# A spectral filter before a mixture of experts: another factoring of the 2496-point transform, and the complex filter product moved out of the third stage's matmul

## The chip, the cores and the metric

The kernel runs on one core of a Trainium2 chip. Times are device microseconds of a whole execution; the median of several executions is the figure. A profile is one execution recorded by the hardware; its span goes from the first to the last recorded instruction and is shorter than the device time.

## The reference, cut to what matters

```python
batch, seq, dim = (8, 2496, 256)          # x; filt_r, filt_i are (1249, 256)
X = np.fft.rfft(x, axis=1)
F = (filt_r + 1j * filt_i)[None, :, :]
y = np.fft.irfft(X * F, n=x.shape[1], axis=1).astype(np.float32)

x = y.reshape(8 * 2496, 256)              # 19968 tokens, 8 experts, F = 1024
logits = x @ w_gate
expert_idx = np.argmax(logits, axis=1)
probs = softmax(logits)                   # gate_w = the chosen expert's
out[n] = gate_w[n] * (np.maximum(x[n] @ w1[e], 0) @ w2[e])    # e = expert_idx[n]
```

Everything is float32.

## The kernel before, in words

It has two halves: the transform with the routing (the first 970 us of the profile), and the experts (the rest). The change is in the first half.

The transform of one batch is written as four stages of matrices. With n = 26 q + t, stage A (`stage_a`, L253) takes 96-point transforms over q, for 26 columns t, two columns (512 numbers a row) to a matmul. Its result goes to a DRAM buffer `zd` and comes back with other rows: 104 = 26 t by 4. Stage B (L266) is a 104 by 104 matrix for each of 24 slots p, 256 columns wide, which gives the coefficients X (real and imaginary parts are rows). VectorE then multiplies X by both parts of the filter, `ht`, in one instruction for a pair of slots (L270, 104 rows by 1024 numbers: P = X Fr and Q = X Fi). Stage C (L281, for the first pair L277) is the back transform over 26 points. It takes P and Q as two matmuls that add up in PSUM, so the complex product's additions and sign changes lie in its matrices, and TensorE does twice the work of one product. ScalarE copies the result out (L282), it goes to the DRAM buffer `ud`, and comes back as 96 rows for stage D (L296), a matrix for each of the 26 columns. D's result `yo` goes to DRAM (`yd`, L312), is transposed on TensorE (L302) and multiplied with the gate weights (L310). When a batch has all its gate products, `route` finds expert, gate and row on VectorE with two matmuls between (L346, L347), and GpSimd scatters (token, gate) to a table in DRAM, one indirect DMA per column: 26 per batch (L368).

A column pair's copies out of PSUM go to ScalarE and VectorE in turn (`evac`, L186 and L188).

The stages of three batches run together: in round b stage B and C of batch b, A of batch b+1 and D of batch b-1, a chunk of four columns or four slots of each in turn (`run_all`). `route` of batch b-1 stands at the end of round b. The program's order on each engine is set when it is built, by a scheduler that estimates times; on the chip every engine takes its own list in order. All loads and stores of the transform are issued by SP; a DMA waits, besides its data, for the DMA issued eight before it on that queue. Input tiles (xt, zi, ui) share 7 buffers, output tiles 5, PSUM banks of the matmuls 5.

The first A chunk is loaded ahead of the constants, the other six behind them: tables, filter (`load_filters`, which copies half of `ht` to its other partitions by DMA, L215), and a fill of the table (L241).

The experts take 128 tokens of one expert at a time: gather by GpSimd (L453), transposes, two matmul layers, a scatter of the result (L502). The first load of the table (L445) waits for all scatters of the routing.

Of the kernel before, what the change touches and what calls it, by code (L numbers as in the profile page):

```python
# [10 lines left out]
F32 = mybir.dt.float32  # L11
# [11 lines left out]
E = 8  # L23
F = 1024
# n = N2*q + t, k = f + N1*g
N1 = 96
N2 = 26
G = N2 // 2
NP = N1 // 4
K2 = 4 * N2  # L30
# [4 lines left out]
def dft_tables():  # L35
    """Matrices of the four transform stages; they depend on the shapes alone.

    Slot s = 24*h + p holds the frequency f = s (0 < s < 48) of the length-96 transforms, and slot 0
    the two real ones, f = 0 and f = 48. A slot's 26 coefficients of the whole transform are at
    k = f + 96*g (u = 0) and k = (96 - f) + 96*g (u = 1), g < 13: all have k <= S/2.  # L40
    """
    q = np.arange(N1)
    t = np.arange(N2)
    g = np.arange(G)
    w = 2.0 * np.pi

    ta = np.zeros((N1, 2, 2, NP))
    td = np.zeros((2, 2, NP, N2, N1))
    n = N2 * q[None, :] + t[:, None]
    for s in range(2 * NP):  # L50
        h, p = divmod(s, NP)
        if s == 0:
            ta[:, h, 0, p] = 1.0
            ta[:, h, 1, p] = (-1.0) ** q
            td[h, 0, p] = 1.0
            td[h, 1, p] = (-1.0) ** q[None, :]
        else:
            ang = w * ((q * s) % N1) / N1
            ta[:, h, 0, p] = np.cos(ang)
            ta[:, h, 1, p] = -np.sin(ang)  # L60
            ang = w * ((n * s) % S) / S
            td[h, 0, p] = np.cos(ang)
            td[h, 1, p] = -np.sin(ang)
    td *= 2.0 / S

    # rows (t, h, c), columns (c', h', u, g)
    tb = np.zeros((N2, 2, 2, NP, 2, 2, 2, G))
    for s in range(2 * NP):
        h, p = divmod(s, NP)
        for u in range(2):  # L70
            k = ((N1 - s if s else N1 // 2) if u else s) + N1 * g
            ang = w * ((t[:, None] * k[None, :]) % S) / S
            c, sn = np.cos(ang), np.sin(ang)
            if s == 0:
                tb[:, h, u, p, 0, h, u] = c
                tb[:, h, u, p, 1, h, u] = -sn
            else:
                i = -1.0 if u else 1.0
                tb[:, h, 0, p, 0, h, u] = c
                tb[:, h, 1, p, 0, h, u] = i * sn  # L80
                tb[:, h, 0, p, 1, h, u] = -sn
                tb[:, h, 1, p, 1, h, u] = i * c
    tb[:, 0, :, 0, 1, 0, 0, 0] = 0.0
    tb[:, 0, 0, 0, 1, 0, 0, 0] = (-1.0) ** t

    # rows (c', h', u, g), columns (t, h, c): of Y itself, generic and with slot 0 in h = 0
    y = np.zeros((2, 2, 2, 2, G, N2, 2, 2))
    for z in range(2):
        for h in range(2):
            for u in range(2):  # L90
                if z and h == 0:
                    k = (N1 // 2 if u else 0) + N1 * g
                    ang = w * ((k[:, None] * t[None, :]) % S) / S
                    y[z, 0, h, u, :, :, h, u] = np.cos(ang)
                    y[z, 1, h, u, :, :, h, u] = -np.sin(ang)
                    if u == 0:
                        y[z, 0, h, u, 0, :, h, u] = 0.5
                        y[z, 1, h, u, 0, :, h, u] = 0.5 * (-1.0) ** t
                else:
                    ang = w * (((g[:, None] + u) * t[None, :]) % N2) / N2  # L100
                    i = -1.0 if u else 1.0
                    y[z, 0, h, u, :, :, h, 0] = np.cos(ang)
                    y[z, 1, h, u, :, :, h, 0] = -np.sin(ang)
                    y[z, 0, h, u, :, :, h, 1] = i * np.sin(ang)
                    y[z, 1, h, u, :, :, h, 1] = i * np.cos(ang)
    # of P = X*Fr and Q = X*Fi, with Yr = Pr - Qi and Yi = Pi + Qr
    yq = np.stack([y[:, 1], -y[:, 0]], axis=1)
    yq[1, :, 0, 0, 0] = 0.0
    tc = np.stack([y, yq], axis=1).reshape(4, K2, K2).transpose(1, 0, 2)

    return {
        "ta": ta.reshape(N1, N1),
        "tb": tb.reshape(K2, NP, K2),
        "tc": tc,
        "td": td.reshape(N1, N2, N1),
    }


@with_exitstack
def kernel(  # L120
# [3 lines left out]
    filt_r: bass.AP,  # L124
    filt_i: bass.AP,
# [6 lines left out]
    td: bass.AP,  # L132
    out: bass.AP,
# [3 lines left out]
    B = x.shape[0]  # L137
    N = B * S
# [5 lines left out]
    zd = [dram.tile([N2, 4, NP, D], F32, tag=f"z{b % 2}", name="zd") for b in range(B)]  # L144
    ud = [dram.tile([N2, 4, NP, D], F32, tag=f"u{b % 2}", name="ud") for b in range(B)]
    yd = dram.tile([N + 1, D], F32, tag="yd", name="yd")
    # Expert e's tokens, in any order, from row e*N on: (token, gate); unused rows hold token N.
# [5 lines left out]
    cnt = perm.tile([N1, E], F32, name="cnt")  # L153
    em8 = perm.tile([N1, E], F32, name="em8")
    eoff = perm.tile([N1, E], F32, name="eoff")
# [8 lines left out]
    tas = cst.tile([N1, N1], F32, name="tas")  # L164
    tbs = cst.tile([K2, NP, K2], F32, name="tbs")
    tcs = cst.tile([K2, 4, K2], F32, name="tcs")
    tds = cst.tile([N1, N2, N1], F32, name="tds")
    ht = cst.tile([K2, 2, NP, D], F32, name="ht")
    wg = cst.tile([P, DH, E], F32, name="wg")
    tri = cst.tile([N1, N1], F32, name="tri")  # L170
    ones = cst.tile([N1, N1], F32, name="ones")
    seg = cst.tile([N1, E, N2], F32, name="seg")
    fill = cst.tile([P, 64, 2], I32, name="fill")
    zrow = cst.tile([1, D], F32, name="zrow")
    ids0 = cst.tile([N1, N2], I32, name="ids0")
    e_i = cst.tile([N1, E], I32, name="e_i")
# [13 lines left out]
    xv = x.rearrange("b (q t) d -> b q t d", t=N2)  # L190
    CH = [(t0, min(4, N2 - t0)) for t0 in range(0, N2, 4)]
    PH = [(p0, 4) for p0 in range(0, NP, 4)]

# [1 line left out]
    nc.sync.dma_start(out=tas, in_=ta)  # L195

    def load_filters():
        nc.sync.dma_start(out=tbs, in_=tb)
        for s, f in enumerate((filt_r, filt_i)):
            for h in range(2):  # L200
                r = 26 * h
                nc.sync.dma_start(
                    out=ht[r:r + G, s],
                    in_=bass.AP(f.tensor, f.offset + NP * h * D, [[N1 * D, G], [D, NP], [1, D]]),
                )
                p0 = 1 - h
                nc.sync.dma_start(
                    out=ht[r + G:r + 2 * G, s, p0:],
                    in_=bass.AP(f.tensor, f.offset + (N1 - NP * h - p0) * D, [[N1 * D, G], [-D, NP - p0], [1, D]]),
                )  # L210
            nc.sync.dma_start(
                out=ht[G:2 * G, s, 0:1],
                in_=bass.AP(f.tensor, f.offset + N1 // 2 * D, [[N1 * D, G], [D, 1], [1, D]]),
            )
            nc.sync.dma_start(out=ht[2 * N2:K2, s], in_=ht[0:2 * N2, s])  # L215
            nc.sync.dma_start(out=ht[2 * N2:2 * N2 + 1, s, 0, :], in_=f[S // 2:S // 2 + 1, :])
        nc.sync.dma_start(out=tcs, in_=tcm)
        nc.sync.dma_start(out=tds, in_=td)
        nc.sync.dma_start(out=wg, in_=moe_w_gate.rearrange("(i p) e -> p i e", p=P))

# [3 lines left out]
        out=tri, in_=ones, compare_op=ALU.is_gt, fill=0.0, base=0, pattern=[[1, N1]], channel_multiplier=-1  # L224
# [6 lines left out]
    nc.gpsimd.iota(ids0, pattern=[[1, N2]], base=0, channel_multiplier=N2)  # L231
# [14 lines left out]
    def stage_a(b):  # L246
        for t0, n in CH:
            xt = sb.tile([N1, 4, D], F32, tag="in", name="xt", bufs=7)
            nc.sync.dma_start(out=xt[:, :n], in_=xv[b, :, t0:t0 + n, :])
            zo = sb.tile([N1, 4, D], F32, tag="st", name="zo", bufs=5)  # L250
            for j in range(0, n, 2):
                ps = bank()
                mm(ps[:N1, :], lhsT=tas, rhs=xt[:, j:j + 2, :], start=True, stop=True)  # L253
                evac(zo[:, j:j + 2, :], ps[:N1, :].rearrange("p (t d) -> p t d", t=2))
            nc.sync.dma_start(out=zd[b].rearrange("t a p d -> (a p) t d")[:, t0:t0 + n, :], in_=zo[:, :n])
            yield

    def stage_bc(b):
        for p0, n in PH:
            zi = sb.tile([K2, 4, D], F32, tag="in", name="zi", bufs=7)  # L260
            nc.sync.dma_start(out=zi[:, :n], in_=zd[b].rearrange("t a p d -> (t a) p d")[:, p0:p0 + n, :])
            uo = sb.tile([K2, 4, D], F32, tag="st", name="uo", bufs=5)
            for j in range(0, n, 2):
                ps = bank()
# [246 lines left out]
    with tc.manual_schedule():  # L511
        for i in range(NT + 5):
# [8 lines left out]
            if 5 <= i:  # L521
                result(i - 5)


_INS = ['x', 'filt_r', 'filt_i', 'moe_w_gate', 'moe_w1', 'moe_w2']


# [18 lines left out]
```

## Time and profile before

| | us |
|---|---|
| median of 3 runs | 2474.87 (2455.88 to 2485.93) |
| span of the profiled execution | 2287.2 (no device time of its own is given; the median is 187.7 above it) |
| first matmul of stage B | 94.7 |
| routing matmuls L346 of batches 0 to 7 | 267.1, 373.1, 478.1, 584.6, 689.7, 798.9, 886.8, 916.8 |
| first transpose of the experts | 970.6 |
| TensorE, VectorE, ScalarE, GpSimd busy | 2006.8, 562.6, 417.6, 519.0 |

The rows of the transform that the change touches, from the groups of instructions (mean of one; a matmul of 512 float32 columns is recorded as two instructions):

| line | operation | count | mean ns |
|---|---|---|---|
| L253 | A, 96x512 | 208 | 706 |
| L266 | B, 104x256 | 384 | 473 |
| L270 | product, VectorE, 104x1024 | 96 | 1225 |
| L281 | C, 104x512 | 352 | 778 |
| L282 | copy, ScalarE, 104x512 | 96 | 586 |
| L296 | D, 96x256 | 416 | 385 |
| L302, L310 | transposes; gate products | 416; 832 | 258; 228 |
| L368 | scatter, GpSimd | 208 | 928 |

How to read it: engines are PE (TensorE), DVE (VectorE), ACT (ScalarE), POOL (GpSimd), SP (issues DMAs). In a list in order of time a line has start, length, engine, source line, operation, tile written and tiles read, and in brackets the idle time of that engine just before, with what ended it. In a table of waits a line has who waited for whom, microseconds in total, times, and the longest. PEclk is the clock granted to TensorE, as a share of full speed.

### The profile page before, as it was taken

The page shows a single profiled execution, that of the slowest core. Times are in us where ns is not written, and L with a number is a line of the kernel's source. Part 1 is how long each engine was busy: PE and PEld are TensorE (multiplying, and loading weights), DVE is VectorE, ACT ScalarE, POOL GpSimd, SP SyncE. Part 2 cuts the span into 40 slices and gives each one's busy share as a digit, 9 for nine tenths or more (in the row PEclk, how much of TensorE's full clock was granted, in tenths as well). Part 3 has the DMA queues.
Part 4 walks back from the last instruction along what each step waited for, and adds up shares of the span by engine and source line. Part 5 has one row for each costly group of instructions (what it writes and reads, how often), then busy time and mean ns, then how long its engine had stood idle before and what let it go on. Part 6 is the DMA issues. An engine that isn't in the chain of part 4 may idle for free. (4 is left out here: it accounts for less than half of the span.)

```text
span 2287.2 us, 25424 instructions
## 1 busy us (share of the span) xinstructions
PE 2006.8 (88%) x8246; PEld 1303.9 (57%) x8246; DVE 562.6 (25%) x911; ACT 417.6 (18%) x750; POOL 519.0 (23%) x550
## 2 busy tenths in 40 slices
PE   0468888888888888099999999999999999999998
PEld 0224444444444446066667776667777667777666
DVE  0122323232323233222222222222222222222221
ACT  0112111111211112012222222222222222222221
POOL 0000122130404042622222222222222222222221
PEclk9898779877977788599999999999999999999999
DMA  8875556563837354611111111111111111111110
GB/s 145 231 222 164 135 155 150 144 158 111 185 113 177 112 128 122 154 32 33 34 36 33 32 33 33 34 36 33 32 33 33 33 35 32 33 33 33 35 34 15
DMA packets 127074, 191.90 MB, mean 84 GB/s; under 512 B 41687, under 2 KB 93603, under 8 KB 126596
## 3 DMA queue, kind: packets, MB, share of 16 engines
q1 hardware_dynamic: 104648, 148.28, 25.9%
q0 software_dynamic: 22304, 42.01, 5.8%
q8 instruction: 75, 1.23, 0.2%
q14 instruction: 47, 0.39, 0.1%
HBM read 104.42 MB, written 84.15 MB: 82 GB/s over the span
## 5 line engine op out<-in xcount | busy, mean ns | idle before, releaser
L475 PE MATMUL hps<-w1s,xT 128*128 x1304 | 589.7, 595 | 1.0 <-DMA idt<-table 0.9
L499 PE MATMUL yps<-w2s,hT 128*128 x2608 | 589.6, 379 | 0.3 <-ACT hT L493 0.3
L499 PEld LDWEIGHTS yps<-w2s,hT 128*128 128x128 f32 x2608 | 495.4, 190 | 137.0 <-issue 77.0
L502 POOL DMA_INDIRECT out_dram<-ys,idt x163 | 165.7, 1016 | 933.4 <-ACT ys L501 933.4
L475 PEld LDWEIGHTS hps<-w1s,xT 128*128 128x128 f32 x1304 | 236.1, 191 | 237.2 <-issue 235.9
L368 POOL DMA_INDIRECT table<-pay,row x208 | 193.1, 928 | 766.5 <-DVE row L365 430.4
L281 PE MATMUL bank<-pq,tcs 104*104 104x512 f32 x352 | 226.6, 778 | 84.1 <-DVE pq L270 84.1
L479 DVE TENSOR_SCALAR h<-hps 128x512 f32<-128x512 f32 x163 | 112.8, 692 | 452.6 <-PE hps L475 452.6
L501 ACT ACTIVATE ys<-yps,idt 128x256 f32<-128x256 f32 x163 | 77.4, 475 | 736.3 <-PE yps L499 736.3
L464 DVE COPY xT<-pt 128x256 f32<-128x256 f32 x163 | 69.2, 425 | 505.7 <-PE pt L462 468.0
L270 DVE TENSOR_TENSOR pq<-bank,ht 104x1024 f32<-104x1024 f32 x96 | 117.6, 1225 | 268.6 <-PE bank L266 253.2
L253 PE MATMUL bank<-xt,tas 96*96 96x512 f32 x208 | 119.3, 706 | 65.5 <-DMA xt<-in_x_dram 65.5
L453 POOL DMA_INDIRECT xg<-yd,idt x163 | 158.2, 971 | 60.2 <-issue 53.0
L489 PE MATMUL pt<-ident,h 128*128 128x128 f32 x1304 | 169.2, 273 | 0.1
L281 PEld LDWEIGHTS bank<-pq,tcs 104*104 104x104 f32 x352 | 63.7, 203 | 176.8 <-DVE pq L270 113.5
L481 ACT ACTIVATE h<-hps 128x512 f32<-128x512 f32 x163 | 97.3, 597 | 317.1 <-PE hps L475 317.1
L266 PE MATMUL bank<-zi,tbs 104*104 104x256 f32 x384 | 133.7, 473 | 22.8 <-DMA zi<-zd 22.8
L282 ACT COPY uo<-bank 104x512 f32<-104x512 f32 x96 | 56.3, 586 | 501.5 <-PE bank L281 395.8
L489 PEld LDWEIGHTS pt<-ident,h 128*128 128x128 f32 x1304 | 147.5, 141 | 0.6 <-DVE h L479 0.4
L491 DVE COPY hT<-pt 128x512 f32<-128x512 f32 x163 | 112.8, 692 | 88.1 <-PE pt L489 88.1
L266 PEld LDWEIGHTS bank<-zi,tbs 104*104 104x104 f32 x384 | 78.9, 218 | 77.8 <-issue 60.8
L253 PEld LDWEIGHTS bank<-xt,tas 96*96 96x96 f32 x208 | 40.5, 198 | 136.0 <-issue 66.2
(76 smaller groups left out, 961.2 us busy)
## 6 DMA issues: line engine op xcount, KB each, us to landing
zi<-zd SPq DMA_DIRECT2D x48, 416.0 KB
ud<-uo SPq DMA_DIRECT2D x48, 416.0 KB
xt<-in_x_dram SPq DMA_DIRECT2D x48, 384.0 KB
zd<-zo SPq DMA_DIRECT2D x48, 384.0 KB
ui<-ud SPq DMA_DIRECT2D x48, 384.0 KB
yd<-yo SPq DMA_DIRECT2D x48, 384.0 KB
w1s<-in_moe_w_dram SPq DMA_DIRECT2D x8, 1024.0 KB
w2s<-in_moe_w_dram SPq DMA_DIRECT2D x8, 1024.0 KB
```

What stands on the lines that cost most here:

```text
L253: mm(ps[:N1, :], lhsT=tas, rhs=xt[:, j:j + 2, :], start=True, stop=True)
L266: mm(ps[:K2, i * D:(i + 1) * D], lhsT=tbs[:, p0 + j + i, :], rhs=zi[:, j + i, :], start=True, stop=True)
L270: nc.vector.tensor_mul(pq, z2[:, None].to_broadcast((K2, 2, 2, D)), ht[:, :, p0 + j:p0 + j + 2, :])
L281: mm(ps[:K2, :], lhsT=tcs[:, s, :], rhs=pq[:, s], start=(s == 0), stop=(s == 1))
L368: sc = nc.gpsimd.indirect_dma_start(out=table, out_offset=bass.IndirectOffsetOnAxis(ap=row[:, t:t + 1], axis=0), in_=pay[:, t, :], in_offs ...
L453: nc.gpsimd.indirect_dma_start(out=xg, out_offset=None, in_=yd, in_offset=bass.IndirectOffsetOnAxis(ap=idt[i].bitcast(U32)[:, 0:1], axis=0))
L475: mm(ps, lhsT=xT[:, dh, :], rhs=w1s[:, bass.ds(ev, 1), dh, fh * 512:(fh + 1) * 512], start=(dh == 0), stop=(dh == DH - 1))
L479: nc.vector.tensor_scalar_max(o, ps, 0.0)
L489: nc.tensor.transpose(pt[:, j, :], h[:, (k + j) * P:(k + j + 1) * P], ident)
L491: nc.vector.tensor_copy(hs[i][:, k:k + 4, :], pt)
L499: mm(ps, lhsT=hT[:, ft, :], rhs=w2s[:, bass.ds(ev, 1), ft, :], start=(ft == 0), stop=(ft == FT - 1))
L502: nc.gpsimd.indirect_dma_start(out=out, out_offset=bass.IndirectOffsetOnAxis(ap=idt.pop(i).bitcast(U32)[:, 0:1], axis=0), in_=ys, in_offse ...
```

## The change

2496 is split as 39 times 64 instead of 96 times 26. With n = 64 q + t, stage A is a 39-point transform, and one matrix of 117 rows does three columns t at once (columns start at T0 = 0, 22 and 43; a group has 22, 21 and 21 of them), so a batch has 22 column groups instead of 26 columns, and 11 matmuls. B has 20 slots (frequencies 0 to 19) instead of 24, with 128 rows: 64 t by real and imaginary part. D is a 117 by 117 matrix for each of 22 groups. The table is scattered to in 22 indirect DMAs per batch, of 117 rows (the last of 39).

The filter product is made whole before stage C: VectorE multiplies with the real part (128 rows by 512 numbers), then crosswise with the imaginary part in two instructions of 64 rows each (imaginary half to real half and back; the sign is in the filter table), and GpSimd adds the two. C is then one matmul of 512 columns for a pair of slots.

x and the filter come in a layout made beforehand on the host: x as (8, 128, 22, 256), rows 117 to 127 unused; the filter as one table of (2, 128, 20, 256), which is loaded in four pieces without copies between partitions. Token numbers and a mask for the empty columns are loaded too.

Loads and stores that go by column groups are cut in three (`columns`: 39 rows each), those by slots in two (64 rows each). Per batch SP issues 6 + 18 + 10 + 10 + 18 + 18 = 80 DMAs (x, zd, zi, ud, ui, yd) instead of 40.

```diff
-N1 = 96
-N2 = 26
+N1 = 39
+N2 = 64
+NF = (N1 + 1) // 2
+T0 = (0, 22, 43)
+NB = len(T0)
+NG = 22
+TP = NB * N1
...
+    def columns(ap, i0, n):
+        for j in range(NB):
+            m = min(n, NC[j] - i0)
+            if m > 0:
+                yield slice(j * N1, (j + 1) * N1), m, ap[T0[j] + i0:T0[j] + i0 + m].rearrange("t s d -> s t d")
...
     def stage_a(b):
-            nc.sync.dma_start(out=xt[:, :n], in_=xv[b, :, t0:t0 + n, :])
+            nc.sync.dma_start(out=xt[:, :n], in_=x[b, :, i0:i0 + n, :])
...
-                mm(ps[:N1, :], lhsT=tas, rhs=xt[:, j:j + 2, :], start=True, stop=True)
+                mm(ps[:TP, :], lhsT=tas, rhs=xt[:TP, j:j + 2, :], start=True, stop=True)
...
-            nc.sync.dma_start(out=zd[b].rearrange("t a p d -> (a p) t d")[:, t0:t0 + n, :], in_=zo[:, :n])
+            for r, m, v in columns(zd[b], i0, n):
+                nc.sync.dma_start(out=v, in_=zo[r, :m])
...
     def stage_bc(b):
-            nc.sync.dma_start(out=zi[:, :n], in_=zd[b].rearrange("t a p d -> (t a) p d")[:, p0:p0 + n, :])
+            nc.sync.dma_start(out=zi[:HP, :n], in_=zd[b][:, f0:f0 + n, :])
+            nc.sync.dma_start(out=zi[HP:, z0:n], in_=zd[b][:, NF - 1 + f0 + z0:NF - 1 + f0 + n, :])
...
-                pq = sb.tile([K2, 2, 2, D], F32, tag="pq", name="pq")
-                nc.vector.tensor_mul(
-                    pq, z2[:, None].to_broadcast((K2, 2, 2, D)), ht[:, :, p0 + j:p0 + j + 2, :]
-                )
+                yv = sb.tile([P, 2, D], F32, tag="yv", name="yv")
+                yw = sb.tile([P, 2, D], F32, tag="yw", name="yw")
+                nc.vector.tensor_mul(yv, z2, ht[:, 0, f:f + 2, :])
+                nc.vector.tensor_mul(yw[:HP], z2[HP:], ht[:HP, 1, f:f + 2, :])
+                nc.vector.tensor_mul(yw[HP:], z2[:HP], ht[HP:, 1, f:f + 2, :])
+                ys = sb.tile([P, 2, D], F32, tag="ysum", name="ysum")
+                nc.gpsimd.tensor_tensor(ys, yv, yw, op=ALU.add)
                 ps = bank()
...
-                    for s in range(2):
-                        mm(ps[:K2, :], lhsT=tcs[:, s, :], rhs=pq[:, s], start=(s == 0), stop=(s == 1))
+                    mm(ps, lhsT=tcs[:, 1, :], rhs=ys, start=True, stop=True)
...
-            nc.sync.dma_start(out=ud[b].rearrange("t a p d -> (t a) p d")[:, p0:p0 + n, :], in_=uo[:, :n])
+            nc.sync.dma_start(out=ud[b][:, f0:f0 + n, :], in_=uo[:HP, :n])
+            nc.sync.dma_start(out=ud[b][:, NF - 1 + f0 + z0:NF - 1 + f0 + n, :], in_=uo[HP:, z0:n])
...
     def stage_d(b):
-            nc.sync.dma_start(out=ui[:, :n], in_=ud[b].rearrange("t a p d -> (a p) t d")[:, t0:t0 + n, :])
+            for r, m, v in columns(ud[b], i0, n):
+                nc.sync.dma_start(out=ui[r, :m], in_=v)
...
-                    mm(ps[:N1, i * D:(i + 1) * D], lhsT=tds[:, t0 + j + i, :], rhs=ui[:, j + i, :],
+                    mm(ps[:k, i * D:(i + 1) * D], lhsT=tds[:k, i0 + j + i, :k], rhs=ui[:k, j + i, :],
...
-            nc.sync.dma_start(out=ytok[:, t0:t0 + n, :], in_=yo[:, :n])
+            for r, m, v in columns(ytok, i0, n):
+                nc.sync.dma_start(out=v, in_=yo[r, :m])
...
     def route(b, lgr):
+        nc.vector.tensor_tensor(idx, idx, vld, op=ALU.mult)
...
-        for t in range(N2):
+        for t in range(NG):
+            k = N1 if t == NG - 1 else TP
             sc = nc.gpsimd.indirect_dma_start(
                 out=table,
-                out_offset=bass.IndirectOffsetOnAxis(ap=row[:, t:t + 1], axis=0),
-                in_=pay[:, t, :],
+                out_offset=bass.IndirectOffsetOnAxis(ap=row[:k, t:t + 1], axis=0),
+                in_=pay[:k, t, :],
```

As built, the order on the engines that the prediction speaks of is this. On TensorE a chunk still reads: C of the second pair, two matmuls of A, four of D, transposes and gate products with the next chunk's B between them, C of the first pair, B of the second pair, C of the second pair. On GpSimd the lists of adds and scatters are: 20 adds, 22 scatters, 11 adds, 22 scatters, 10, 22, 9, 22, 10, 22, 10, 22, 10, 22, and the last 22 scatters. Before, GpSimd had scatters alone.

## The prediction

> **What bounds the kernel now.** I read the page's first two parts, then busy time by stretches, then the table of waits, and then the instructions in order of time inside one round of the transform.
>
> ```profile
> span 2287.2 us, 25424 instructions
> ...
> PE 2006.8 (88%) x8246; PEld 1303.9 (57%) x8246; DVE 562.6 (25%) x911; ACT 417.6 (18%) x750; POOL 519.0 (23%) x550
> ...
> PE   0468888888888888099999999999999999999998
> ...
> PEclk9898779877977788599999999999999999999999
> ```
>
> TensorE is the busy engine in both halves. From slice 17 on it runs the experts at 99% and full clock; nothing there is touched. What can move lies in slices 0 to 16, where it is busy 8 tenths and its granted clock lies between 0.7 and 0.9. Columns below: stretch, length, busy time of each engine, granted clock, DMA share, GB/s.
>
> ```profile
> 168.00:267.00 99.00, 82.91 (x334) 46.47 (x334) 28.45 (x39) 18.95 (x33) 0.00 (x0) 0.84 0.51 150
> 268.00:373.00 105.00, 89.10 (x337) 48.17 (x335) 33.37 (x49) 17.23 (x32) 24.10 (x26) 0.79 0.57 147
> ...
> 917.00:970.00 53.00, 1.47 (x4) 0.73 (x4) 9.77 (x24) 0.00 (x0) 33.67 (x37) 0.50 0.69 161
> ```
>
> One round (B and C of one batch, A of the next, D of the one before) is some 105 us: the routing matmuls (L346) start at 267.1, 373.1, 478.1, 584.6, 689.7, 798.9, 886.8 and 916.8, so rounds 2 to 6 take 106.3 each, round 7, without A, 88, round 8, D alone, 30. DMA is half idle; TensorE stands still for 16 us of a round. The waits say for what:
>
> ```profile
> POOL table L368 <- DVE row L365: 430.4, 7, 77.2
> ...
> PE bank L281 <- DVE pq L270: 84.1, 73, 1.4
> ```
>
> So of 96 pairs of slots 73 make TensorE wait for the product. In order of time this is:
>
> ```profile
> 499.21 0.92 POOL L368 DMA_INDIRECT table<-pay,row  x1 [0.30 <-issue]
> ...
> 500.44 0.92 POOL L368 DMA_INDIRECT table<-pay,row  x1 [0.30 <-issue]
> ...
> 515.22 1.91 PE L266 MATMUL bank<-zi,tbs 104*104 104x256 f32 x4
> ...
> 517.17 1.22 DVE L270 TENSOR_TENSOR pq<-bank,ht 104x1024 f32<-104x1024 f32 x1 [6.67 <-PE bank L266]
> ...
> 518.45 3.74 PE L281 MATMUL bank<-pq,tcs 104*104 104x512 f32 x4 [1.32 <-DVE pq L270]
> ...
> 521.98 3.40 PE L253 MATMUL bank<-xt,tas 96*96 96x512 f32 x4
> ...
> 525.22 1.89 PE L296 MATMUL bank<-ui,tds 96*96 96x256 f32 x8
> ...
> 536.55 1.96 PE L281 MATMUL bank<-pq,tcs 104*104 104x512 f32 x4 [1.32 <-DVE pq L270]
> ```
>
> Three things to see. TensorE takes its list in order: behind L266 of a chunk's second pair comes L281 of the same pair with nothing between, so the wait (1.32) is the product (1.22) and a hop. The same work comes in two speeds: L281 3.74 or 1.96, L266 1.91 (1.03 at 527.5), L253 3.40 or 1.88: half and full clock. And a scatter costs GpSimd 1.226 us from start to start (0.92 and 0.30).
>
> **The change, part by part.** I work per round (one batch through each stage), because the rounds repeat, and against the profiled span. The page gives that execution no time but its span, 2287.2; the median run, 2474.87, lies 187.7 above it (the runs 168.7 to 198.7). I carry the 187.7 over unchanged.
>
> **TensorE's work.** A goes from 13 to 11 matmuls of 512 columns (0.94 each), B from 24 to 20 of 256 (0.5), C from 24 to 10 of 512 (0.9), D from 26 to 22 of 256 (0.47), transposes and gate products from 52 to 44 each (0.14 and 0.2). At full clock a round loses 1.9 + 2.0 + 12.6 + 1.9 + 1.1 + 1.6 = 21 us.
>
> **The wait per pair.** The one product of 1.22 becomes three of 512 columns on VectorE and an add on GpSimd, one behind the other. A 512-column VectorE pass from PSUM is 0.69 (L188, L479), and two in a row take 1.50, so three take 2.3. No add on GpSimd is in the trace. Its nearest rows are memsets, 172 ns for 96 elements and 276 for 208: 0.93 ns an element and 83 ns. One stream of 512 elements would be 0.56, three 1.5; I take the two inputs, 1.04. With hops of 0.03 to 0.28 (iota to VectorE, VectorE to scatter) the chain is 3.6 (3.1 to 4.1). The new kernel's list on TensorE has the same shape: the second pair's C stands directly behind its B, so it waits all 3.6; the first pair's has a gate product and its wait in between (1.2), so 2.4.
>
> Only a page prices such an add: the Trainium skill, "GPSIMD Engine Reference", section 3.1, has 4497 ns for 2048 fp32 elements, an estimate of 1.12 for 512, which would add 0.08 a pair, some 6 us in all.
>
> **The scatters in front of the add.** Until now GpSimd had nothing in the transform but scatters, and no one waited for them before the end. Now its list is 20 adds, 22 scatters, 11 adds, 22 scatters, and so on. The scatters of batch b stand before the adds of batch b+2, and TensorE, with C next in its list, stands behind those. From the routing matmul to the row numbers is 5.3 (267.1 to 272.5 without the product that lay between), then 0.28, 22 scatters at 1.226 = 27.0, the add and its hop 1.2: 33.8; TensorE has the routing matmuls and B (3.4) in it. It stands still 30.4 us, in rounds 2 to 7. Queued behind it are A and D of that round; on SP, the stores of their results. Where the first pair's add gets ahead of the scatters, the second is caught: the same.
>
> **One chunk (two pairs, four columns of A and D).** C, A, D in one stretch: 0.9 + 1.88 + 1.89 = 4.7 at full clock, 8.7 at half. Transposes, gate products and the next B: 4.0 (507.8 to 511.7 now), 6.5 at half. Wait 2.4. C and B: 1.9 or 3.7. Wait 3.6. Sum 16.6 at full clock, 24.7 at half. Which clock? In the trace the clock falls after the stretch of transposes and gate products though its gaps are 0.7 at most, holds in round 0 (0.95 from 95 to 160 us) with waits of 1.32 in every 4 to 6 us, and comes back only when a stretch has run dense for some 4 to 6.8 us (530.8 to 535.3; 518.45 to 525.2). Waits of 2.4 and 3.6 around 1.9 of work will drop it in nearly every chunk. I let C, A, D start slow for 5.1 us (then 2.1 more: 7.2) and C and B be slow half the time (2.8): 7.2 + 4.0 + 2.4 + 2.8 + 3.6 = 20.0. Now a chunk takes 17.1.
>
> The rule for this clock speaks against the change as well: the Trainium skill, "TensorE: Matmul & The Clock Gate", section "HAM oscillation — how this bites in real kernels", wants no idle gap over about 3.4 us. The trace is stricter, since it drops the clock with gaps of 0.7; by the page alone only the wait of 3.6 would count, a chunk would be 19.1, and the whole some 32 us less.
>
> **Rounds 2 to 6.** Five chunks 100, less one wait of 2.4, plus 30.4, plus 5.5 for the odd columns and route (10.9 now from the last D to the routing, less a regular 5.4), plus 3.4 for routing and B: 137, against 106.3: +31 each, +155. Round 7, without A on both sides: +35. Round 1, no scatters ahead: 109 against 99.3, +10. Round 0: five chunks of B, wait, C twice and A are 12.9 at full and 18.1 at half clock; with 0.9 and the 9.2 that the loads cost now, 75 to 101 against 73.1; I take 91, +18.
>
> **Ends.** SP waits over 30 us on copies inside the filter load (L215, L216; 120 to 180 GB/s move meanwhile); the new load is 8.4 MB in long rows without such waits, and the rows of 66 to 95 us show 234 to 295 GB/s: the inputs of A come at 35 to 45 instead of 66. Bounds 0 and -32, I take -20. At the end GpSimd issues 44 scatters instead of 52 from 893.4 on, which is what the 53 us of the third stretch are made of: -9 (-6 if a scatter of 117 rows is slower).
>
> **DMA.** SP issues 80 transfers a round instead of 40, of half the size, 0.3 to 0.6 us each; 40 more are 16 us of SP, which is idle most of a round. But each waits for the one issued eight before, and in the list the third load of some ui comes behind stores of the same chunk's zo: D waits 3 to 5 us (at 264.2 a load of zi took 5.0 from issue to use). One such per round is 4 x 7 = +28; bounds 0 and +70. VectorE's two products more per pair (80 x 0.85 = 68 us) cost nothing beside the chain: VectorE is busy 33 of 105; what of them is on the path is in the chain already. Nothing is counted for the padded rows of x (128 rows of 22 columns instead of 2496: +0.3 MB a round, DMA being half idle), the sign change of the filter at the start (behind the load) and one more small product in the routing (0.17 a round).
>
> Sum: 155 + 35 + 10 + 18 - 20 - 9 + 28 = +217. 2474.87 + 217 = 2692, say 2690. All at full clock, no DMA wait, the cheap add: +3; all at half clock, the dear add, all DMA waits: +500.
>
> **Rivals.** (1) TensorE's work is the bound and the waits hide. For it: TensorE is at 85% in a round. Against: its list has nothing to put between B and C. It would give 2475 - 8 x 21 - 29 = 2278. It decides if the waits of a round grow by less than 25 us; I count 5 x 3.6 + 4 x 2.4 + 30 = 58 against 12 now, so they grow by 46. (2) The clock holds: work dense enough at 4.7 us a stretch to get back to full at once: +41, 2516. For it: round 0 holds it today. Against: its waits are 1.32. (3) The clock stays down, and SP's order costs several waits a round: 2840 and up to 2930. For it: the third stretch shows 0.50 when TensorE idles, and C, A, D must be unbroken to win it back; a late ui breaks it.
>
> **How the numbers follow.** My forecast (2570 to 2840) 0.70; rival 2 (2500 to 2570) 0.10; rival 3 (2840 to 2970) 0.13; rival 1 0.07. About 2% is what a measurement of this kernel can tell from no change, 2425 to 2524. Rival 1 complete is faster, 0.03; partly, within 2%, 0.04, and 0.01 of rival 2's lower end. Slower 0.92. For 8 in 10 the range goes half way into rivals 2 and 3 (0.05 each): 2535 to 2880.
>
> **What would show it.** The add's row at 1.0 to 1.1 us; a wait of TensorE for it of 450 us in all (80 times, 2 to 4 each, six of about 30); six groups of GpSimd's 22 scatters, each with TensorE idle beside it; L306 at 80 to 90 matmuls with half the present busy time of C; a clock near 0.7 in slices 2 to 16; first B near 75 us. Wrong if GpSimd's scatters run beside adds, if the long waits are not there, or if the clock in a round is above 0.85.

## The result, and the profile after

| | before | changed |
|---|---|---|
| median, us | 2465.38 (2454.81 to 2485.93, 4 runs) | 2679.77 (2677.44 to 2682.56, 4 runs) |
| ratio | 1 | 1.0861, 95% interval 1.0804 to 1.0918: slower |
| profiled execution | span 2287.2, no time of its own | time 2682.56, span 2680.9 |

Forecast: 2690. The number is right, in part by luck, as the account below shows. The last row does not fit the forecast's frame: the changed kernel's span lies 1.7 us below its time, so nothing like 187.7 us lies around a span, and by the two profiles the kernel lost 394 us, not 214. That had to be settled first (experiment 1).

The page of the changed kernel, its first two parts:

```profile
span 2680.9 us, 25028 instructions
...
PE 1975.8 (74%) x7654; PEld 1307.4 (49%) x7654; DVE 601.0 (22%) x1057; ACT 397.6 (15%) x718; POOL 599.8 (22%) x597
...
PE   2555356454645536365369999999999999999998
...
PEclk6666666665656656566579999999999999999999
```

TensorE went from 8 tenths to 5 in the transform and its clock from 0.7-0.9 to 0.6. It does less work and is hardly less busy. Rounds 2 to 6 of the changed kernel in one stretch (length, busy time of PE, PEld, DVE, ACT, POOL, clock, DMA share, GB/s):

```profile
307.00:1099.00 792.00, 413.52 (x1320) 239.16 (x1320) 185.71 (x341) 78.31 (x142) 171.02 (x160) 0.62 0.40 102
```

and the same rounds in the first profile of before:

```profile
267.00:799.00 532.00, 452.66 (x1691) 248.21 (x1692) 165.16 (x255) 89.59 (x162) 119.86 (x130) 0.79 0.59 145
```

That is 158.5 us a round for 106.4, TensorE busy 82.7 of it for 90.5, where 21 us less was worked out at full clock. What TensorE waits for (who for whom, us in total, times, longest):

```profile
PE bank L306 <- POOL ysum L300: 227.5, 70, 3.7
PE bank L304 <- issue: 90.2, 3, 30.1
...
PE bank L306 <- issue: 51.6, 2, 25.8
PE bank L304 <- POOL ysum L300: 46.3, 5, 30.2
```

All four lines are the wait of C for the sum, 416 us; "issue" stands where the profile names no releaser. The long waits, of 25 us and more, are called holds below. The start of round 2 in order of time, with the end of the row of scatters:

```profile
312.45 0.68 DVE L298 TENSOR_TENSOR yw<-bank,ht 64x512 f32<-64x512 f32 x1
...
337.40 0.98 POOL L410 DMA_INDIRECT table<-pay,row  x1 [0.30 <-issue]
338.69 0.90 POOL L410 DMA_INDIRECT table<-pay,row  x1 [0.30 <-issue]
339.61 1.27 POOL L300 TENSOR_TENSOR ysum<-yv,yw 128x512 f32<-128x512 f32 x1
...
340.93 2.08 PE L304 MATMUL bank<-ysum,tcs 128*128 128x256 f32 x4 [30.24 <-POOL ysum L300]
```

The products are done at 313.1; the add starts at 339.6, behind 22 scatters, and TensorE stands still for 30.24. The groups of GpSimd:

```profile
L300 POOL TENSOR_TENSOR ysum<-yv,yw 128x512 f32<-128x512 f32 x80 | 100.9, 1261 | 845.9 <-DVE yw L298 824.0
...
L410 POOL DMA_INDIRECT table<-pay,row x176 | 173.8, 987 | 176.4 <-DVE row L406 125.2
```

### The profile page after: what moved, and what is told of

It reads as the page before. It is cut to its first block, busy times and chain, and to the rows that moved or that the text cites. A ratio compares the mean times of both kernels' runs of the same rounds, so it can differ in the third digit from the quotient of the medians.

```text
span 2680.9 us, 25028 instructions
## 1 busy us (share of the span) xinstructions
PE 1975.8 (74%) x7654; PEld 1307.4 (49%) x7654; DVE 601.0 (22%) x1057; ACT 397.6 (15%) x718; POOL 599.8 (22%) x597
## 5 line engine op out<-in xcount | busy, mean ns | idle before, releaser
L306 PE MATMUL bank<-ysum,tcs 128*128 128x512 f32 x144 | 146.5, 1120 | 279.1 <-POOL ysum L300 227.5
L300 POOL TENSOR_TENSOR ysum<-yv,yw 128x512 f32<-128x512 f32 x80 | 100.9, 1261 | 845.9 <-DVE yw L298 824.0
L410 POOL DMA_INDIRECT table<-pay,row x176 | 173.8, 987 | 176.4 <-DVE row L406 125.2
L306 PEld LDWEIGHTS bank<-ysum,tcs 128*128 128x128 f32 x144 | 34.8, 300 | 314.4 <-POOL ysum L300 261.3
L273 PE MATMUL bank<-xt,tas 117*117 117x512 f32 x176 | 137.2, 928 | 64.5 <-DMA xt<-in_x_dram 64.5
L291 PE MATMUL bank<-zi,tbs 128*128 128x256 f32 (+1 forms) x320 | 138.2, 561 | 36.2 <-DMA zi<-zd 32.1
L325 PE MATMUL bank<-ui,tds 117*117 117x256 f32 (+1 forms) x352 | 117.9, 481 | 60.6 <-DMA ui<-ud 21.0
L307 ACT COPY uo<-bank 128x512 f32<-128x512 f32 x80 | 46.8, 585 | 763.9 <-PE bank L306 551.8
L296 DVE TENSOR_TENSOR yv<-bank,ht 128x512 f32<-128x512 f32 x80 | 55.3, 691 | 414.4 <-PE bank L291 409.0
L325 PEld LDWEIGHTS bank<-ui,tds 117*117 117x117 f32 (+1 forms) x352 | 79.0, 236 | 110.3 <-issue 91.8
```

What stands on the lines that cost most here:

```text
L273: mm(ps[:TP, :], lhsT=tas, rhs=xt[:TP, j:j + 2, :], start=True, stop=True)
L291: mm(ps[:, i * D:(i + 1) * D], lhsT=tbs[:k, f + i, :], rhs=zi[:k, j + i, :], start=True, stop=True)
L300: nc.gpsimd.tensor_tensor(ys, yv, yw, op=ALU.add)
L306: mm(ps, lhsT=tcs[:, 1, :], rhs=ys, start=True, stop=True)
L325: mm(ps[:k, i * D:(i + 1) * D], lhsT=tds[:k, i0 + j + i, :k], rhs=ui[:k, j + i, :], start=True, stop=True)
L410: sc = nc.gpsimd.indirect_dma_start(out=table, out_offset=bass.IndirectOffsetOnAxis(ap=row[:k, t:t + 1], axis=0), in_=pay[:k, t, :], in_of ...
```

## Experiments

The median of before was 2458 to 2468 in the three sets below. "Round" is the mean of rounds 2 to 6; busy and clock are TensorE's in them. "3 at a time" is experiment 3's way of issuing scatters. A number in the kernel column means the kernel of that experiment. "Late loads" are waits of TensorE for xt, zi or ui after the first 60 us.

| | kernel | us | ratio to before (95%) | round | busy | clock |
|---|---|---|---|---|---|---|
| 1 | before, second profile | 2474 | - | 129.7 | 94.5 | 0.72 |
| | changed | 2680 | 1.086 (1.080 to 1.092) | 158.5 | 82.7 | 0.62 |
| 2 | changed, add on VectorE | 2546 | 1.035 (1.027 to 1.042) | 141.3 | 83.2 | 0.65 |
| 3 | changed, scatters 3 at a time | 2577 | 1.048 (1.040 to 1.055) | 141.2 | 83.8 | 0.65 |
| 4 | new factoring, old product | 2476 | 1.009 (1.005 to 1.013) | 131.1 | 81.7 | 0.76 |
| 5 | before, 3 at a time | 2327 | 0.941 (0.935 to 0.948) | 107.2 | 91.3 | 0.78 |
| 6 | 4, 3 at a time | 2385 | 0.965 (0.958 to 0.971) | 115.4 | 78.0 | 0.80 |
| 7 | 2, 3 at a time | 2467 | 1.004 (1.000 to 1.008) | 126.4 | 82.2 | 0.66 |
| 8 | 3, C later | 2349 | 0.952 (0.946 to 0.958) | 115.7 | 70.9 | 0.74 |
| 9 | 8, x on ScalarE's queue | 2241 | 0.908 (0.902 to 0.915) | 100.9 | 65.1 | 0.77 |
| 10 | 6, x on ScalarE's queue | 2327 | 0.947 (0.939 to 0.954) | 111.2 | 76.3 | 0.81 |
| 11 | 5, C later | 2157 | 0.875 (0.868 to 0.881) | 82.4 | 75.1 | 0.91 |
| 12 | before, two rows of 13 | 2467 | 1.001 (0.996 to 1.006) | | | |

**1. Before, once more.** No edit.

> The kernel before, unchanged, with a second profile. Its first profile has a span of 2287.2 us and a granted clock of 0.917, but its device times are 2454.8 to 2485.9; the changed kernel's span lies only 1.7 below its device time. Theory A, the first recorded execution was granted a higher clock than the timed ones: device time 2455 to 2486 again, span within 3 us of it, clock 0.84 to 0.89, rounds 2 to 6 at 120 to 130 us instead of 106.3, waits of TensorE as before (84 us for the product). Theory B, the record leaves out some 178 us ahead of or behind the span: span 2287 again beside a device time near 2465, clock 0.917, rounds 106. Theory C, the kernel has two speeds in any execution: this one falls on 2287 or on 2465 with device time and span together.

Time 2474.38, span 2472.7, clock 0.877: span and time together, so theory B falls, and of A the clock is only a part. Its rounds and new waits:

```profile
274.00:922.00 648.00, 472.54 (x1690) 258.82 (x1690) 164.50 (x253) 89.45 (x162) 119.52 (x130) 0.72 0.48 119
```

```profile
PE bank L281 <- DVE pq L270: 103.3, 69, 18.9
PE lg L310 <- issue: 77.7, 11, 12.2
...
PE lg L310 <- ACT yt L186: 35.9, 17, 13.3
```

The first profile has 84.1 for the product, longest 1.4, 11.1 for yt and no second line. In order of time, some 15 us after the row's first scatter (281.86):

```profile
295.47 1.03 PE L266 MATMUL bank<-zi,tbs 104*104 104x256 f32 x4
...
295.91 0.69 DVE L188 COPY yo<-bank 96x512 f32<-96x512 f32 x1 [0.88 <-PE pt L302]
...
302.94 0.48 ACT L186 COPY yt<-pt 128x384 f32<-128x384 f32 x1 [8.83 <-remote]
...
312.60 0.92 POOL L368 DMA_INDIRECT table<-pay,row  x1 [0.30 <-issue]
312.74 1.22 DVE L270 TENSOR_TENSOR pq<-bank,ht 104x1024 f32<-104x1024 f32 x1 [16.14 <-remote]
```

The product at 312.74 waits for nothing but the matmul of 295.47, whose (modelled) end is 296.5; VectorE has been idle since 296.6. "remote" means that a semaphore did rise, at a moment when the profile knows nobody who raised it. So what VectorE and ScalarE need from TensorE reaches them 7 to 16 us late in the rows shown (2 to 19 in all of this profile), until the row of 26 scatters is through. Such delays, and the clock that they lower, are what an ordinary execution has and the first profile lacked. Against this profile the changed kernel loses 208 us of span, 29 a round.

**2. The add on VectorE.**

```diff
-                nc.gpsimd.tensor_tensor(ys, yv, yw, op=ALU.add)
+                nc.vector.tensor_tensor(ys, yv, yw, op=ALU.add)
```

> The changed kernel with the add of the two products on VectorE, so that GpSimd has scatters alone. Theory 1 (the add costs twice: 3.7 us of chain per pair, and six times some 30 us behind the scatters): the six holds go (6 x 30 = -180), a pair's chain is shorter by 0.57 (0.69 for 1.26) and a hop of 0.2, 80 x 0.75 = -60: 2440, between 2400 and 2490; waits of TensorE for the sum 2.9 and 1.7 us, 190 us in all instead of 416, none over 6. Rival, the clock (waits of over 2 us keep it low, and that is the loss): the same waits, but the clock in the rounds stays at 0.60 to 0.66 and TensorE's busy time per round stays near 84, so rounds of 115 or more; if it came back to 0.8 a round would be near 100 and the time 2370. Rival, the order of SP's 80 transfers: the holds only hid late loads, time falls by less than 100, to 2580 or more, and waits for ui, xt and zi grow by 15 us a round.

2546, 134 less than the changed kernel, not 240 less: theory 1 is half of it. The 30 us holds are gone. But now TensorE runs on beside the row of scatters and meets the delays of experiment 1 (28.4 us of waits at L348 without a releaser and 23.9 for yt, longest 14.7; one wait for the sum is 11.8). The waits for the sum and product are still 250 us in all, and the clock stays at 0.65: the rival on the clock was right.

**3. Scatters three at a time.** `route` puts its scatters on a list, and each add of a later round lets three go:

```diff
+        pending.extend((scatter, t) for t in range(NG))
...
-                nc.gpsimd.tensor_tensor(ys, yv, yw, op=ALU.add)
+                ad = nc.gpsimd.tensor_tensor(ys, yv, yw, op=ALU.add)
+                some(3, ad.ins.name)
```

> The changed kernel with a batch's 22 scatters kept back and issued three at a time behind each add of a later round, add still on GpSimd. Theory 1: only the holds go: 6 x 30 = -180, some 0 to 0.5 us more at a second pair's add that stands behind three scatters (3.9 us), +0 to +20, so 2510, between 2480 and 2550; TensorE's longest wait for the sum under 6 us, the usual ones as now (3.7 and 2.4 to 3.0), 240 to 270 us in all. Rival, a lower clock is what costs: the same -180, and rounds 1 and 2 to 6 alike at 125 to 135 with clock 0.62 to 0.66, still longer than before's 106 although TensorE does less. Rival, transfers are late anyway: less than -80.

2577: 103 less, not 180. The holds are gone (longest wait for the sum 4.0), but the waits for the sum grow from some 235 outside the holds to 266, since an add may stand behind three scatters, and waits for late loads from 120 to 155: in a hold loads had caught up. 181 less 31 less 35 is 115. Delays of TensorE's results are left in round 8 alone (one of 13.5 us), where there are no more adds and a batch's 22 scatters go in one row. Rounds 2 to 6:

```profile
308.00:1014.00 706.00, 418.90 (x1320) 243.56 (x1320) 184.92 (x344) 78.45 (x142) 171.65 (x160) 0.65 0.45 114
```

**4. The new factoring with the old product.** One VectorE instruction for both parts, C as two accumulating matmuls, the second with its matrix's halves exchanged:

```diff
-                nc.vector.tensor_mul(yv, z2, ht[:, 0, f:f + 2, :])
...
-                nc.gpsimd.tensor_tensor(ys, yv, yw, op=ALU.add)
+                nc.vector.tensor_mul(pq, z2[:, None].to_broadcast((P, 2, 2, D)), ht[:, :, f:f + 2, :])
...
-                    mm(ps, lhsT=tcs[:, 1, :], rhs=ys, start=True, stop=True)
+                    for s in range(2):
+                        mm(ps, lhsT=tcs[:, 2 * s + 1, :], rhs=pq[:, s], start=(s == 0), stop=(s == 1))
```

> The changed kernel with the old form of the filter product: one VectorE instruction for both parts (128 rows by 1024), no add, and C as two matmuls of 512 columns that add up in PSUM, the second with its matrix's halves exchanged. So the new factoring alone is left. Theory 1 (the moved product is the whole loss, the factoring a gain): C costs 10 x 0.9 = 9 us a round more than in the changed kernel at full clock, the wait is 1.3 per pair, 105 us in all, no holds: against before a round loses 12 us of TensorE's work and gains some 3.5 of late loads, 8 x -8.5 - 20 at the start = -88: 2380, between 2330 and 2430. Rival, the factoring with its 80 transfers a round costs by itself: 2520 or more, with waits for ui, xt and zi of 20 us a round. Rival, the clock: waits of 1.3 hold it at 0.75 to 0.85 in the rounds; if it falls to 0.65 here as well, waits are not what lowers it.

2476, between the two theories. It has the delays too (44.3 and 18.2 us of waits without a releaser, 17.9 for yt), and late loads of 160 us. Its clock of 0.76 is what the third theory wanted of waits of 1.3.

**5 to 7. Before, 4 and 2 with scatters three at a time,** here behind the product or the add on VectorE, so that GpSimd waits for it.

```diff
-                nc.vector.tensor_mul(
+                ad = nc.vector.tensor_mul(
...
+                some(3, ad.ins.name)
```

> The kernel before, with a batch's 26 scatters kept back and issued three at a time, each group waiting for the product of a slot pair of a later round. Theory (in the second profile of before, VectorE and ScalarE start 7 to 16 us after TensorE's matmul, again and again from some 15 us after the first scatter of a row of 26 to its end; a long row of scatters makes this): waits of TensorE named issue and for yt fall from 127 us to under 25, rounds 2 to 6 from 129.7 to 106 to 112, time 2290 to 2340. Rival, the delay has another cause than the row (the number of scatters, or something that comes and goes): rounds of 120 or more, time 2430 to 2480.

> The new factoring with the old product (one VectorE instruction, C doubled) as in the run before, and scatters three at a time behind each product. Theory: the delays of 7 to 16 us go, some 105 us; waits for late loads (100 us for ui and xt in front of D, 48 for zi) stay: 2370, between 2330 and 2400, rounds 2 to 6 near 118, clock there 0.72 to 0.80. Against before with its scatters spread this is the factoring alone: theory 1 (a gain of 12 us of TensorE's work a round) wants it lower by 50 or more; the rival, the 80 transfers a round eat the gain, wants it equal or higher.

> The changed kernel with the add on VectorE and scatters three at a time behind each add. Theory: waits for the sum stay (2.9 and 1.7 to 2.4 us, some 210 to 240 us in all), the delays go (28 + 25 + some 20 us): 2470, between 2430 and 2500, rounds near 130, clock 0.62 to 0.68. Against the doubled C with spread scatters, this is the product alone: some 100 slower although TensorE does 9 us less a round. If it comes out as fast or faster, the chain in front of C is not what costs.

2327, 2385 and 2467, all three inside their ranges. Before is 6% faster with not an instruction less: its rounds are the first profile's (107.2 and 106.4) and the waits at L310 (now L311) without a releaser are 1.0 us. Two lines of its waits:

```profile
PE bank L282 <- DVE pq L270: 81.5, 71, 1.4
...
PE lg L311 <- ACT yt L186: 11.1, 18, 0.6
```

Here too one delay is left, 16.6 us in round 8, beside a row that is not split. So a long row makes it. Without it the change comes apart in clean steps. The factoring alone: 2327 to 2385, a loss of 58, though TensorE is busy 13 us less a round; its late loads (180 us of waits for ui, zi and xt, where experiment 5 has 24) take more than that, as the rival said: 22 us a round in rounds 2 to 6. Another 17 lie behind the last routing and have another cause (see "Tail" below); the earlier start gives 27 back. The product alone, with the add on VectorE: 2385 to 2467, a loss of 81, though C has half the matmuls; busy time per round rises from 78.0 to 82.2, because the clock goes from 0.80 to 0.66. With the add on GpSimd (experiment 3) it is another 110; there the scatters stand behind the add by the list's order alone, so two things differ. Added up, 58, 81, 110 and the 103 of the holds lead from 2327 to the changed kernel's 2680; before pays 141 for its own rows of 26.

**8. C later.** Experiment 3 with C of a chunk put behind B of the next chunk:

```diff
-                ys = sb.tile([P, 2, D], F32, tag="ysum", name="ysum")
+                ys = sb.tile([P, 2, D], F32, tag="ysum", name="ysum", bufs=5)
...
+                sums.append((j, ys))
+            if held:
+                back(*held)
+            held = f0, n, z0, sums
             yield
+        back(*held)
+        yield
```

> The changed kernel with its add on GpSimd and scatters three at a time behind each add, and with C of a chunk's two pairs put behind B of the next chunk's (five buffers for the sum instead of two), so that A and D lie between a pair's B and its C. Theory 1 (the loss is the wait of TensorE for the chain, and the clock that it lowers): waits for the sum fall from 266 us to under 40, TensorE's clock in the rounds goes from 0.64 to 0.75 or more, its busy time per round from 84 to 72 to 77, time 2577 less 230 less 60: 2290, between 2250 and 2350. Rival, the clock stays at 0.64 without these waits: 2340 to 2360, busy time per round still 84. Rival, SP's order: late loads take over, waits for ui, xt and zi grow from 155 to over 250: 2430 or more.

2349, at the upper end of theory 1's range. The time alone would also fit the rival with a clock of 0.64 (2340 to 2360); clock and busy time decide against it. No wait for the sum is left in the table. The same matmuls as in experiment 3 keep TensorE busy 70.9 instead of 83.8 us a round, the clock is 0.74 instead of 0.65:

```profile
227.00:806.00 579.00, 354.50 (x1328) 222.64 (x1328) 189.40 (x348) 78.36 (x142) 173.52 (x161) 0.74 0.60 141
```

What takes the sum's place is, as the rival on SP's order said, a load:

```profile
PE bank L273 <- DMA xt<-in_x_dram: 192.9, 21, 12.1
```

**9 and 10. The loads of x on ScalarE's queue,** in 8 and in 6.

```diff
-            nc.sync.dma_start(out=xt[:, :n], in_=x[b, :, i0:i0 + n, :])
+            nc.scalar.dma_start(out=xt[:, :n], in_=x[b, :, i0:i0 + n, :])
```

> The run with C later, with the loads of x issued by ScalarE's queue instead of SP's. There TensorE waited 193 us for x in front of A (21 times, up to 12.1). Theory 1 (those loads stand on SP behind stores that wait for their data, in a queue of 80 transfers a round): the waits for x fall under 60 us, rounds 2 to 6 from 115.7 to 100, clock 0.78 or more: 2220, between 2180 and 2270. Rival (they wait for a free one of the seven input tiles, whoever issues them): waits for x stay over 140 us, 2320 to 2350.

> The new factoring with the old product, scatters three at a time, and the loads of x on ScalarE's queue. There D waited 114 us for ui (46 of them with a load of x landing last), B 66 for zi. Theory 1 (SP's order is what the factoring costs): those waits fall by 60 or more, 2320, between 2280 and 2345, now at or below before with its scatters spread (2327). Rival (the split transfers themselves are late, data or buffers): 2365 to 2400.

2241 and 2327, inside both ranges. In 9 the waits for x are gone: they were SP's order, not a lack of tiles. But the waits for ui and zi grow, from 22 and 36 to 126 and 116. In rounds 2 to 6 late loads of all three fall only from 39.5 to 31.4 us a round; TensorE's busy time, 5.8 less, gives most of the rest of the 14.8. In 10 the waits for loads did not fall (133 us in front of D instead of 114, 53 in front of B instead of 66); so its theory failed though the time is in its range. Where its 58 come from is not shown (23 of them lie ahead of the first routing, 21 in rounds 2 to 6).

**11. Before with both.** Experiment 5 with C of a pair behind B of the next pair (`pq` with three buffers instead of two).

> The kernel before with scatters three at a time and C of a slot pair put behind B of the next (three buffers for the product instead of two). Theory 1 (a wait in front of every C costs its length and lowers the clock besides): the 95 us of waits for the product fall under 20, the clock in the rounds rises from 0.79 to 0.85 or more, TensorE's busy time per round falls from 88 to 80, rounds from 107 to 95: 2327 less 75 less 50 gives 2200, between 2170 and 2245. Rival, the clock does not depend on these waits: busy 88 as before, 2245 to 2265. Rival, the waits only move to the loads: 2300 or more.

2157, better than the range. The waits for the product fall from 92 to 0.6 us, clock and rounds:

```profile
229.00:641.00 412.00, 375.73 (x1692) 224.98 (x1691) 164.44 (x253) 89.59 (x162) 119.88 (x130) 0.91 0.72 187
```

For the same matmuls TensorE is busy 75.1 instead of 91.3 us a round. The waits themselves were 10.6 a round in experiment 5, so the clock was worth more than the waits. This is the fastest version of all: 2157 where before takes 2461 and the changed kernel 2680.

**12. Before, two rows of 13.** `some(13, ...)` instead of `some(3, ...)`.

> The kernel before with a batch's 26 scatters in two rows of 13, the first behind the product of a later round's first pair and the second behind that of the next pair. Theory A (the delay of TensorE's completions begins some 15 us, 12 scatters, after a row's first one, and the second row follows the first almost at once, since a pair comes each 8 us and a row takes 16): much of it stays, 2400 to 2470. Theory B (any pause lets the backlog go): 2325 to 2350. Together with rows of 3 (2327) and of 26 (2468) it says how long a row may be.

2467, as before, but it is no test of a row of 13: for one batch GpSimd issued 18, paused for 1.6 us and issued 8, for the others 26 without a break. Experiment 11 says more. Its scatters came in rows of 9, 6 and 3, and beside three of its four rows of 9 in the rounds a result came late. One of them, whose first scatter starts at 401.65:

```profile
407.77 0.53 PE L314 MATMUL pt<-ident,yo 96*128 96x96 f32 x4
...
411.45 0.92 POOL L380 DMA_INDIRECT table<-pay,row  x1 [0.30 <-issue]
412.30 0.48 ACT L186 COPY yt<-pt 128x384 f32<-128x384 f32 x1 [5.35 <-remote]
412.84 1.45 PE L322 MATMUL lg<-wg,yt 128*96 128x8 f32 x8 [3.67 <-issue]
```

The transposes end at 408.3, ScalarE's copy starts 4.0 us later, and TensorE stands still for 3.67; beside the other two the copy is 2.7 and 4.7 late. Beside rows of 6 or 3, here and in experiment 5, there are no such starts. So a row of 9 is already too long, and less so than one of 18 or 26.

## Why the prediction was right, point by point

Against the second profile of before the span grew by 208; the forecast's sum was +217.

- **Start**, -20: first B at 67.2 for 93.1, -26.
- **Rounds 0 and 1**, +28: from the first B to the first routing 239.7 for 181.0, +59. The clock did not hold in round 0 either.
- **Rounds 2 to 6**, +155 and 18 of the DMA term: 158.5 for 129.7, +144. **Round 7**, +35: 135.9 for 115.5, +20.
- **Tail**, -9: round 8 and what follows take 128.2 for 119.5, +9. From the last routing to the experts' first transpose it is 66.6 for 52.7. The last row of scatters did become shorter, 29 us for 39, though a scatter of 117 rows takes 1.29 from start to start for 1.226. But the experts' first load of the table starts 20.5 us behind it, for 1.8. Ahead of that load SP has the eight loads of w2s, the second layer's weights; before, they went out from 1107.1 on, beside the scatters, and in the changed kernel they wait for the scatters and start at 1334.2:

```profile
SPq L480 <- DMA table<-pay,row: 24.6, 1, 24.6
```

  All nine kernels here with the new factoring have these 20 to 23 us, the five profiles of before and its forms 2 to 4. The forecast had no term for it.
- **The add**, 1.04: 1.26. **The chain**, 3.6 and 2.4: 3.66, and 2.4 to 2.96. **The hold**, 30.4 in rounds 2 to 7: 30.24, 30.1 three times, and twice 4.45 with 25.8. In all 416 us for 450 forecast. These steps were right; removing the holds (experiment 3) and the chain (8) showed that both cost. The recorded chunk at half clock adds up to 24.9, not 24.7; only the upper bound of +500 rests on it.
- **Two steps failed and cancelled; that the number came out is luck to that extent.** "I carry the 187.7 over unchanged" took for something outside the span what was delays and a lower clock in the rounds of the second profile and, by their times, of the other executions. The changed kernel does not pay them in its rounds: TensorE stands in the hold while the row of scatters runs. So its gain on before's real rounds was overlooked, 23 us a round (129.7 for 106.4). It meets them in round 8 alone (one wait of 12.4). On the other side a new round was forecast at 140.5 with its share of the DMA term and took 158.5: chunks took 21.8 with load waits taken off where 20.0 was forecast (some 9 a round), and late loads were 108 us (without the first wait for zi) for 11, where +28 was forecast and +70 was its bound (68 of them in rounds 2 to 6, another 10 a round).
- **The clock.** The forecast let waits of 2.4 and 3.6 lower the clock, and that held: 0.62, also in round 0, which has no transposes and gate products. Its reading of before, that "the clock falls after the stretch of transposes and gate products", named half of the cause. Experiment 11 keeps that stretch, lacks the waits of 1.3 in front of C, and runs at 0.91. But the waits alone do not lower the clock either: round 0 of before has twelve of them in 65 us and no such stretch, and runs at 0.95 (in both profiles of before and in experiment 5):

```profile
95.00:160.00 65.00, 47.78 (x126) 21.39 (x125) 19.50 (x19) 10.53 (x18) 0.00 (x0) 0.95 0.72 228
```

  In before's rounds, which have both, it is 0.79. So the waits of 1.3 already cost clock there, together with the stretch, and that was missed; why the two together do it is not shown. The Trainium skill, "TensorE: Matmul & The Clock Gate", section "HAM oscillation — how this bites in real kernels", wants no idle gap over some 3.4 us. In rounds 2 to 6 of experiment 5 no wait of TensorE is longer than 2.5 and those for the product are 1.3, yet taking the latter away raised the clock from 0.78 to 0.91. Here the measurement decides: gaps well under that limit can cost clock.
- **The rivals.** Rival 1 was wrong. Rival 2, that the clock holds, was wrong. Rival 3 has most of its mechanism (0.62 and several load waits a round) and not its price, because its base was off by the delays.

## What to carry to other kernels

A wait in front of a matmul can be paid twice, once as itself and once as a lower clock for what follows, as it was in rounds 2 to 6 here; putting other matmuls between producer and consumer (experiments 8 and 11) was worth more than halving the consumer's work. Before moving arithmetic to an engine, read what else stands in that engine's list: 22 scatters of 1.29 us stood in front of each batch's first or second add. And compare a profile's span with the times of other executions before building on it: where they differ by 8%, that profile does not show the executions that are timed.

## What was not expected of the hardware

- A long row of indirect scatters without a pause (0.92 us each, 0.30 between) makes results of TensorE reach VectorE and ScalarE late: by 2 to 19 us beside rows of 26 (experiment 1), by 2.7 to 4.7 beside rows of 9, the earliest some 6 us after the row's start. Three at a time with pauses between do not: 2468 to 2327 in before. In every profile but the first, all starts in the transform that the profile gives to "remote" after over 1 us of idle time lie beside a row of eight or more, or at most some 5 us behind one. Whether the matmuls finish late or only their semaphores rise late can't be seen (matmul ends are modelled), and what in the row causes it was not tried. Why the first profile has none of it stays open: the other executions of before took 2436 to 2488.
- The add of two 128x512 float32 tiles takes GpSimd 1.26 us; the same add takes VectorE 0.69 (experiment 2). The Trainium skill, "GPSIMD Engine Reference", section 3.1, scaled to 512 gave an estimate of 1.12; it measured 12% more.
